# A cross network's first layer as one sequence of twelve half-blocks

## Chip, cores, metric

One core of one Trainium2 chip. The metric is the device time of one execution in microseconds (us), as the median of several runs; lower is better.

## The reference

A cross network of six layers over a batch of 4096 rows with 416 features, all in bf16:

```
x = x0                                   # (4096, 416)
for l in range(6):
    x = x0 * (x @ ws[l] + bs[l]) + x     # ws[l]: (416, 416), bs[l]: (416,)
```

Each layer is a product with a 416 x 416 matrix, a bias, a product with the input x0 and a sum with the layer's own input.

## The kernel before

**Tiling.** The 416 features are three blocks of 128 (`NK`, the index `m` for outputs and `k` for inputs) and a remainder of 32. In the first five layers features lie on the partitions and batch rows on the free axis. The batch is two halves `s` of 2048 rows, each of four groups `g` of 512 columns; two groups make a half-block `h` (1024 columns). `XM[0]` holds x0 transposed (three blocks), `XR[0]` its remainder with the four groups `g` at partitions 32g, and `XRd` a copy of `XR[0]` with the upper and the lower 64 partitions exchanged. `XM[1]`, `XM[2]`, `XR[1]`, `XR[2]` take the layers' outputs in turn.

**Forms of product on TensorE.** A full matmul has 128 x 128 weights and 512 columns (L233). A row-tiled product has 32 input rows (the remainder) and 128 outputs; four of them, at the four groups of 32 rows of the array, run side by side (L240, L206). A column-tiled product has 128 input rows and 32 outputs; again four run side by side (L200, L212, L217). The kernel writes the place in the array as `tile_position`.

**The first layer** (`first_layer(s)`, L227 to L291), called for each half of the batch. A half-block of one feature block `m` needs 3 full matmuls (k = 0 to 2) for each of its two groups (`full`) and 2 row-tiled products (`row`). They accumulate in one PSUM tile of two banks; the pool has four such tiles. `pa` are the three half-blocks with h = 0, `pb` those with h = 1. In each half of the batch the row-tiled products come at two places: eight of them after `pa` is filled, four at the end. The remainder outputs (`mm_rem`, 16 column-tiled products per half) come at the end of the second half.

An evicted half-block goes through ACT (bias added, PSUM to a buffer `t` in SBUF, six buffers, L173), then VectorE (times x0, L180; plus the layer's input, L183).

**What is loaded, and how.** SP's queue issues eight transposing DMAs for x0 (`load_x0t`, L75), one for each group of 512 rows, then the other weights. ACT's queue issues the first layer's weights (L71), the biases (L105), the remainder of the first half of x0 in four pieces (`xrig`, L83) and the remainder rows of the first layer's weights (`WR`, L91). L111 is a small activation that has ACT load its function table. Two copies on ACT (L115) and one on GpSimd (L117) spread `WR` to the other groups of partitions. `xrig` is transposed on TensorE (`x0_rem0`, L159) and copied by VectorE to `XR[0]` and `XRd`. The remainder of the second half (`xrem`, 2048 pieces of 64 bytes, L88) is loaded later: `load_xrem1` is called at the end of `x0_rem0`, and a one-column memset of `xrem` on VectorE (L86), behind those copies, holds the load back. VectorE transposes `xrem` into `XR[0]` (L167) and fills `XRd` by two copies (L169), in `x0_rem1`.

**Order.** A scheduler orders the instructions of each engine from the program's order and its own estimates. `pin(...)` keeps an instruction in the program's order on its engine. Each DMA takes one of eight semaphores in turn, and waits until the transfer that had it before has landed.

**After the first layer,** layers 1 to 4 run over six tiles each (`mm_full`, `mm_row`, L200 and L206) with one pair of remainder products per layer; the last layer puts the batch on the partitions (L365 to L392) and stores the outputs.

Of the kernel before, what the change touches and what calls it, by code (L numbers as in the profile page):

```python
# [9 lines left out]
ACT = mybir.ActivationFunctionType  # L10
ALU = mybir.AluOpType
BF16 = mybir.dt.bfloat16
# [4 lines left out]
def kernel(  # L17
# [7 lines left out]
    nc = tc.nc  # L25
    B, D = x0.shape
    L = ws.shape[0]
    P = 128
# [38 lines left out]
    def col0(s, g):  # L67
        return SW * s + CW * g
# [8 lines left out]
    def pin(ins):  # L77
        tc.keep_in_program_order(ins)
# [4 lines left out]
                nc.scalar.dma_start(xrig[:, i, :].rearrange("p (g r) -> p g r", g=NG), x0_v[:, i:16:4, NK * P:D])  # L83

    def load_xrem1():
        pin(nc.vector.memset(xrem[:, 0, 0:1], 0.0))  # L86
        with nc.allow_non_contiguous_dma(reason="64B row segments"):
            pin(nc.scalar.dma_start(xrem[:], x0[SW:2 * SW, NK * P:D].rearrange("(p t) r -> p t r", p=P)))  # L88

# [18 lines left out]
    load_x0t(0, 1)  # L108
    load_xrem0()
    load_wr0()  # L110
    nc.scalar.activation(dz[:, 1:2], dz[:, 0:1], ACT.Identity, bias=dz[:, 0:1], scale=1.0)  # L111
    for g in range(1, NG):
        dst, src = WR[32 * g:32 * g + 32, 0, :], WR[0:R, 0, :]
        if g < NG - 1:
            nc.scalar.copy(dst, src)  # L115
        else:
            nc.gpsimd.tensor_copy(dst, src)  # L117
    for g in range(2, NG):
        load_x0t(0, g)
    load_x0t(1, 0)  # L120
# [17 lines left out]
    fill_wd(0, 1)  # L138
    fill_wd(1, L)

    wps = psum.tile([P, CW], FP32, tag="ps", name="wps")

# [13 lines left out]
    def x0_rem0(tpr):  # L156
        nc.tensor.transpose(tpr[:, CW:CW + L], bsb[0:L, NK * P:4 * P], ident[0:L, 0:L])
        for i in range(4):
            nc.tensor.transpose(tpr[:, 128 * i:128 * i + 128], xrig[:, i, :], ident[:])  # L159
        for dst, src in ((slice(0, P), slice(0, P)), (slice(64, P), slice(0, 64)), (slice(0, 64), slice(64, P))):  # L160
            to = XR[0] if dst == src else XRd
            pin(nc.vector.tensor_copy(to[dst, 0:CW], tpr[src, 0:CW]))
        nc.vector.tensor_copy(bR[:], tpr[:, CW:CW + L])
        load_xrem1()

    def x0_rem1():
        pin(nc.vector.transpose(XR[0][:, CW:2 * CW].rearrange("p (j t) -> p t j", t=16), xrem[:]))  # L167
        for dst, src in ((slice(64, P), slice(0, 64)), (slice(0, 64), slice(64, P))):
            pin(nc.vector.tensor_copy(XRd[dst, CW:2 * CW], XR[0][src, CW:2 * CW]))  # L169

    def ew_act(n, pt, bias):
        t = tpool.tile([P, 2 * CW], BF16, name="t")
        nc.scalar.activation(t[:, 0:n], pt, ACT.Identity, bias=bias, scale=1.0)  # L173
        return t

    def ew_main(l, s, m, h, pt, cur, nxt, pin_all=False, t=None):
        c0 = col0(s, 2 * h)
        if t is None:
            t = ew_act(2 * CW, pt[:].rearrange("p a b -> p (a b)"), bM[:, m, l:l + 1])
        prod = nc.vector.tensor_tensor(out=t[:], in0=t[:], in1=XM[0][:, m, c0:c0 + 2 * CW], op=ALU.mult)  # L180
        if pin_all:
            pin(prod)
        total = nc.vector.tensor_tensor(out=nxt[:, m, c0:c0 + 2 * CW], in0=t[:], in1=cur[:, m, c0:c0 + 2 * CW], op=ALU.add)  # L183
        if pin_all and s:
            pin(total)

    def ew_rem(l, s, pr, curR, nxtR, pin_all=False, t=None):
        tr = ew_act(CW, pr, bR[:, l:l + 1]) if t is None else t
        prod = nc.vector.tensor_tensor(out=tr[:, 0:CW], in0=tr[:, 0:CW], in1=XR[0][:, CW * s:CW * s + CW], op=ALU.mult)  # L189
        if pin_all:  # L190
            pin(prod)
        total = nc.vector.tensor_tensor(out=nxtR[:, CW * s:CW * s + CW], in0=tr[:, 0:CW], in1=curR[:, CW * s:CW * s + CW], op=ALU.add)  # L192
        if pin_all:
            pin(total)

    def mm_full(l, s, m, g, pts, cur, first, last):
        c0 = col0(s, g)
        for k in range(NK):
            for q in range(4):
                nc.tensor.matmul(pts[g // 2][32 * q:32 * q + 32, g % 2, :], lhsT=WM[:, l, k, 128 * m + 32 * q:128 * m + 32 * q + 32],  # L200
                                 rhs=cur[:, k, c0:c0 + CW], start=(first and k == 0), stop=(last and k == NK - 1),
                                 tile_position=(0, 32 * q))

    def mm_row(l, s, m, pts, curR, first, last):
        for g in range(NG):
            nc.tensor.matmul(pts[g // 2][:, g % 2, :], lhsT=WR[32 * g:32 * g + 32, l, 128 * m:128 * m + 128],  # L206
                             rhs=curR[32 * g:32 * g + 32, CW * s:CW * s + CW],
                             start=first, stop=last, tile_position=(32 * g, 0))

    def mm_rem(l, s, pr, cur, curR):  # L210
        for g in range(NG):
            nc.tensor.matmul(pr[32 * g:32 * g + 32, :], lhsT=WD[:, l, g, :], rhs=curR[:, CW * s:CW * s + CW],  # L212
                             start=True, stop=False, tile_position=(0, 32 * g))
        for k in range(NK):
            for g in range(NG):
                c0 = col0(s, g)
                nc.tensor.matmul(pr[32 * g:32 * g + 32, :], lhsT=WM[:, l, k, NK * P:D], rhs=cur[:, k, c0:c0 + CW],  # L217
                      start=False, stop=(k == NK - 1), tile_position=(0, 32 * g))

    def new_pts():  # L220
        return [psum.tile([P, 2, CW], FP32, tag="ps", name=f"pt{h}") for h in range(2)]
# [2 lines left out]
        nc.sync.dma_start_transpose(out=XLrows[:, 16 * s:16 * s + 16, 128 * k:128 * k + 128],  # L224
                                    in_=nxt[:, k, SW * s:SW * s + SW])

    def first_layer(s):  # L227
        cur, curR, nxt, nxtR = XM[0], XR[0], XM[1], XR[1]

        def full(pt, m, h, gl, after_row):  # L230
            c0 = col0(s, 2 * h + gl)
            for k in range(NK):
                nc.tensor.matmul(pt[:, gl, :], lhsT=WM[:, 0, k, 128 * m:128 * m + 128], rhs=cur[:, k, c0:c0 + CW],  # L233
                                 start=(k == 0 and not after_row), stop=(k == NK - 1 and after_row))

        def row(pt, m, h, opens):
            for gl in range(2):
                rg = 32 * ((2 * h + gl) ^ (2 if m == 1 else 0))
                src = XRd if m == 1 else curR
                nc.tensor.matmul(pt[:, gl, :], lhsT=WR[rg:rg + 32, 0, 128 * m:128 * m + 128],  # L240
                                 rhs=src[rg:rg + 32, CW * s:CW * s + CW],
                                 start=opens, stop=not opens, tile_position=(rg, 0))

        def ph(m):
            return psum.tile([P, 2, CW], FP32, tag="ps", name=f"ph{m}")

        pa = [ph(m) for m in range(NK)]
        if s == 0:
            for m in range(NK):
                full(pa[m], m, 0, 0, False)  # L250
            tp0 = psum.tile([P, CW + 8], BF16, tag="ps", name="tpr")
            x0_rem0(tp0[:])
            for m in range(NK):
                full(pa[m], m, 0, 1, False)
        else:
            for gl in range(2):
                for m in range(NK):
                    full(pa[m], m, 0, gl, False)
        pb = [ph(0)]
        row(pa[0], 0, 0, False)  # L260
        row(pb[0], 0, 1, True)
        row(pa[2], 2, 0, False)
        row(pa[1], 1, 0, False)
        for m in range(NK):
            ew_main(0, s, m, 0, pa[m], cur, nxt, pin_all=(s == 1))
        for m in range(NK):
            if m:
                pb.append(ph(m))
            for gl in range(2):
                full(pb[m], m, 1, gl, m == 0)  # L270
        row(pb[1], 1, 1, False)
        row(pb[2], 2, 1, False)
        if s == 0:
            x0_rem1()
            for m in range(NK):
                ew_main(0, s, m, 1, pb[m], cur, nxt, pin_all=True)
            return
        pr = psum.tile([P, 2, CW], FP32, tag="ps", name="pr")
        for r in range(NS):
            mm_rem(0, r, pr[:, r, :], cur, curR)  # L280

        def act_main(m):
            return ew_act(2 * CW, pb[m][:].rearrange("p a b -> p (a b)"), bM[:, m, 0:1])

        tb, tr = [act_main(0), act_main(1)], [ew_act(CW, pr[:, 0, :], bR[:, 0:1])]
        tb.append(act_main(2))
        tr.append(ew_act(CW, pr[:, 1, :], bR[:, 0:1]))
        ew_rem(0, 0, None, curR, nxtR, True, tr[0])
        for m in range(NK):
            ew_main(0, s, m, 1, None, cur, nxt, True, tb[m])  # L290
        ew_rem(0, 1, None, curR, nxtR, True, tr[1])  # L291

    bias_setup()
    pe_filler(1, CW)
    for s in range(NS):
        first_layer(s)

    def rem_pair(l, cur, curR, nxtR, feeds_last):
        pr2 = psum.tile([P, 2, CW], FP32, tag="ps", name="pr2")
# [154 lines left out]
```

## Time and profile before

| | |
|---|---|
| runs | 130.0, 130.21, 130.25 us; median 130.21 |
| profiled execution | 130.03 us, of which its span is 128.2 us |
| granted TensorE clock, mean | 0.995 |
| x0 transposes issued by SP | 0.73 to 17.1 us |
| first matmul on x0 | 5.61 us |
| row-tiled products of the first layer start | 10.57, 15.19, 19.51, 24.04 us |
| first matmul of layer 1 | 26.11 us |
| first eviction of the first layer on ACT | 11.00 us |

Times in the profile count from the start of the span. A line of a group names the source line, the engine and the operation. The clock that the array was granted is full all through but for the last slices. Matmuls are pipelined, so one takes 0.38 us while its neighbours start 0.216 us apart.

### The profile page before, as it was taken

The numbers are of one execution on the slowest core, as the hardware profiler recorded it, in microseconds if no ns is written. First come the engines' busy times: TensorE is split into PE (matmuls) and PEld (weight loads), VectorE is DVE, ScalarE is ACT, GpSimd is POOL, SyncE is SP. The second block draws the span as 40 slices with busy tenths as digits, with TensorE's granted clock in tenths as the row PEclk, the third lists the DMA queues.
The fourth block names the chain that finished last, engine by engine and source line by source line (L and its number), as shares of the span: only waits on it lengthen the run. The fifth ranks groups of instructions, "written<-read, shape, count | busy, mean of one in ns | idle before, by whom it ended". The sixth has DMA issues, their size and how long they took to land.

```text
span 128.2 us, 3995 instructions
## 1 busy us (share of the span) xinstructions
PE 122.7 (96%) x1698; PEld 55.1 (43%) x1698; DVE 108.1 (84%) x196; ACT 86.8 (68%) x99; POOL 5.5 (4%) x18
## 2 busy tenths in 40 slices
PE   7999999999999999999999999999999999999960
PEld 3344343444344444434444434444434445445420
DVE  0033999999999999999999989898989899898991
ACT  0138857878496658857658857658857897569670
POOL 4004000700000000000000000000000000000000
PEclk9999999999999999999999999999999999999997
DMA  3999999999960000000000000000297899987754
GB/s 93 248 233 196 193 222 251 279 332 332 337 202 0 5 0 8 0 0 5 0 5 0 5 0 5 0 0 5 48 160 165 161 134 240 182 269 248 224 183 136
DMA packets 42230, 16.38 MB, mean 128 GB/s; under 512 B 31034, under 2 KB 42212, under 8 KB 42212
## 3 DMA queue, kind: packets, MB, share of 16 engines
q1 hardware_dynamic: 37432, 15.40, 52.8%
q10 hardware_dynamic: 4780, 0.72, 3.7%
q8 instruction: 13, 0.21, 0.7%
q14 instruction: 5, 0.04, 0.1%
HBM read 6.15 MB, written 3.41 MB: 75 GB/s over the span
## 4 chain that ended last, share of the span: by engine, by line
PE 81%; DVE 6%; DMA 6%; ACTq 2%; issue 1%; SPq 1%; ACT 1%; DVEq 0%
PE pt L200 50%; PE ph L233 11%; PE pt L206 5%; PE pr L217 5%; PE py L365 4%; DMA xrig<-in_x_dram 4%; DVE t L393 4%; DVE o L382 2%; DMA out_dram<-o 2%; PE pr L212 2%; PE ph L240 1%; PE py L360 1%; ACTq L83 1%; SPq L383 1%; PE py L371 1%
## 5 line engine op out<-in xcount | busy, mean ns | idle before, releaser
L200 PE MATMUL pt<-XM,WM 128*32 128x512 bf16 x1152 | 65.2, 379 | 0.0
L173 ACT ACTIVATE t<-pt,bM 128x1024 bf16<-128x1024 f32 x48 | 49.6, 1115 | 17.7 <-PE pt L206 17.7
L183 DVE TENSOR_TENSOR XM<-t,XM 128x1024 bf16<-128x1024 bf16 x60 | 41.5, 692 | 3.6
L180 DVE TENSOR_TENSOR t<-t,XM 128x1024 bf16<-128x1024 bf16 x60 | 41.4, 689 | 3.5 <-ACT t L173 3.4
L200 PEld LDWEIGHTS <-WM 128*32 128x32 bf16 x1152 | 29.7, 97 | 33.8 <-issue 5.1
L392 ACT CAST t<-py 128x416 bf16<-128x416 f32 (+1 forms) x23 | 14.8, 643 | 4.7 <-PE py L365 2.5
L233 PE MATMUL ph<-XM,WM 128*128 128x512 bf16 x72 | 16.4, 379 | 0.3 <-DMA XM<-in_x_dram 0.3
L365 PE MATMUL py<-WM,XM 128*128 128x416 bf16 x90 | 16.5, 339 | 0.0
L173 ACT ACTIVATE t<-ph,bM 128x1024 bf16<-128x1024 f32 x12 | 12.6, 1113 | 3.5 <-PE ph L240 3.5
L365 PEld LDWEIGHTS <-XM 128*128 128x128 bf16 x90 | 8.5, 98 | 7.8 <-issue 1.4
L393 DVE TENSOR_TENSOR t<-t,X0rows 128x416 bf16<-128x416 bf16 (+1 forms) x23 | 10.4, 456 | 1.1 <-ACT t L392 1.1
L233 PEld LDWEIGHTS <-WM 128*128 128x128 bf16 x72 | 6.8, 98 | 8.8 <-issue 1.3
L382 DVE TENSOR_TENSOR o<-t,XLrows 128x416 bf16<-128x416 bf16 (+1 forms) x23 | 10.4, 455 | 0.0
L173 ACT ACTIVATE t<-pr,bR 128x512 bf16<-128x512 f32 x10 | 6.4, 685 | 2.9 <-PE pr L217 2.9
L217 PE MATMUL pr<-XM,WM 128*32 128x512 bf16 x120 | 8.2, 379 | 0.0
L206 PE MATMUL pt<-XR,WR 32*128 32x512 bf16 x96 | 7.3, 379 | 0.0
L111 ACT ACT_TABLE_LOAD x1 | 1.3, 1283 | 6.0 <-DMA XM<-in_x_dram 6.0
L192 DVE TENSOR_TENSOR XR<-t,XR 128x512 bf16<-128x512 bf16 x10 | 4.2, 424 | 0.7
L217 PEld LDWEIGHTS <-WM 128*32 128x32 bf16 x120 | 3.2, 97 | 3.2
L145 PE MATMUL wps<-const-float32-1.0 128*128 128x512 f32 x4 | 3.6, 1044 | 0.8 <-PEq L438 0.8
L189 DVE TENSOR_TENSOR t<-t,XR 128x512 bf16<-128x512 bf16 x10 | 4.2, 419 | 0.0
L154 DVE CAST bM<-pb 128x18 f32<-128x18 bf16 x1 | 0.2, 177 | 4.5 <-PE pb L153 4.5
(42 smaller groups left out, 36.7 us busy)
## 6 DMA issues: line engine op xcount, KB each, us to landing
X0rows<-in_x_dram SPq DMA_DIRECT2D x8, 312.0 KB, 7.1
out_dram<-o SPq DMA_DIRECT2D x9, 208.0 KB, 4.2
WM<-in_ws_dram SPq DMA_DIRECT2D x5, 312.0 KB
out_dram<-o SPq DMA_DIRECT2D x13, 104.0 KB, 1.7
X0rows<-in_x_dram SPq DMA_DIRECT2D x4, 208.0 KB, 6.1
WR<-in_ws_dram SPq DMA_DIRECT2D x4, 130.0 KB, 5.2
WM<-in_ws_dram ACTq DMA_DIRECT2D x1, 312.0 KB
XM<-in_x_dram SPq DMA_TRANSPOSE x8, 5.6
```

The lines of the kernel that those rows point to most:

```text
L173: nc.scalar.activation(t[:, 0:n], pt, ACT.Identity, bias=bias, scale=1.0)
L180: prod = nc.vector.tensor_tensor(out=t[:], in0=t[:], in1=XM[0][:, m, c0:c0 + 2 * CW], op=ALU.mult)
L183: total = nc.vector.tensor_tensor(out=nxt[:, m, c0:c0 + 2 * CW], in0=t[:], in1=cur[:, m, c0:c0 + 2 * CW], op=ALU.add)
L189: prod = nc.vector.tensor_tensor(out=tr[:, 0:CW], in0=tr[:, 0:CW], in1=XR[0][:, CW * s:CW * s + CW], op=ALU.mult)
L200: nc.tensor.matmul(pts[g // 2][32 * q:32 * q + 32, g % 2, :], lhsT=WM[:, l, k, 128 * m + 32 * q:128 * m + 32 * q + 32], rhs=cur[:, k, c0:c ...
L206: nc.tensor.matmul(pts[g // 2][:, g % 2, :], lhsT=WR[32 * g:32 * g + 32, l, 128 * m:128 * m + 128], rhs=curR[32 * g:32 * g + 32, CW * s:CW ...
L217: nc.tensor.matmul(pr[32 * g:32 * g + 32, :], lhsT=WM[:, l, k, NK * P:D], rhs=cur[:, k, c0:c0 + CW], start=False, stop=(k == NK - 1), tile ...
L233: nc.tensor.matmul(pt[:, gl, :], lhsT=WM[:, 0, k, 128 * m:128 * m + 128], rhs=cur[:, k, c0:c0 + CW], start=(k == 0 and not after_row), sto ...
L365: nc.tensor.matmul(py[:, 0:D], lhsT=cur[:, k, q_cols(q, g)], rhs=WM[:, l, k, :], start=((not closes) and k == 0), stop=(closes and k == NK ...
L382: tc.keep_in_program_order(nc.vector.tensor_tensor(out=o, in0=t, in1=xl, op=ALU.add))
L392: nc.scalar.copy(tv, src)
L393: tc.keep_in_program_order(nc.vector.tensor_tensor(out=tv, in0=tv, in1=X0rows[:, b, :], op=ALU.mult))
```

## The change

- The first layer becomes one function without the loop over halves: twelve half-blocks in one sequence, `pa[0..2]`, `pb[0..2]` (first half of the batch), `qa[0..2]`, `qb[0..2]` (second half).
- Row-tiled products come at three places of eight: behind `pa` (as before); behind the full matmuls of `pb[1]`, `pb[2]` and of the first groups of `qa[0]`, `qa[1]`; and behind those of `qa[2]` and `qb[0]`, where they open `qb[1]` and `qb[2]`.
- `qb[1]` and `qb[2]` are column-tiled (`cols`): 24 products of 32 outputs for each, in place of 6 full matmuls. The remainder products follow them.
- `load_xrem1` loses its memset and is called right behind the small activation, ahead of the copies of `WR`. The activation and the copies are pinned.
- `x0_rem1` (transpose of `xrem` and two copies) moves ahead of VectorE's work on `pa[1]` and `pa[2]`.
- Evictions are issued one by one (`act_main`, `act_rem`), all pinned, and the remainder's evictions come behind all others. The matmuls of the first layer from the first row-tiled place on, those of its remainder, and the first tile of layer 1 are pinned.

In the order of instructions that comes out, ACT's queue holds the table load, the small activation, the load of `xrem` (waiting on the semaphore of the first `xrig` load), then the copies of `WR`. SP's list is the same but for the semaphores of three transposes and of the loads behind them. TensorE has 36 products more.

The core of the diff:

```diff
     def load_xrem1():
-        pin(nc.vector.memset(xrem[:, 0, 0:1], 0.0))
...
-    nc.scalar.activation(dz[:, 1:2], dz[:, 0:1], ACT.Identity, bias=dz[:, 0:1], scale=1.0)
-    for g in range(1, NG):
-        dst, src = WR[32 * g:32 * g + 32, 0, :], WR[0:R, 0, :]
...
+    pin(nc.scalar.activation(dz[:, 1:2], dz[:, 0:1], ACT.Identity, bias=dz[:, 0:1], scale=1.0))
+    load_xrem1()
...
+        copy_wr0()
         for dst, src in ((slice(0, P), slice(0, P)), (slice(64, P), slice(0, 64)), (slice(0, 64), slice(64, P))):
...
-        load_xrem1()
...
-    def first_layer(s):
+    def first_layer():
...
+        def cols(pt, s, m, h, gl):
+            c0 = col0(s, 2 * h + gl)
+            for k in range(NK):
+                for q in range(4):
+                    pin(nc.tensor.matmul(pt[32 * q:32 * q + 32, gl, :], lhsT=WM[:, 0, k, 128 * m + 32 * q:128 * m + 32 * q + 32],
+                                         rhs=cur[:, k, c0:c0 + CW], start=False, stop=(k == NK - 1), tile_position=(0, 32 * q)))
...
+        row(pa[0], 0, 0, 0, ())
+        row(pb[0], 0, 0, 1, (0, 1))
+        row(pa[2], 0, 2, 0, ())
+        row(pa[1], 0, 1, 0, ())
+        dve_main(0, 0, 0, act_main(pa[0], 0))
+        x0_rem1()
+        for m in range(1, NK):
+            dve_main(0, m, 0, act_main(pa[m], m))
+        for gl in range(2):
+            full(pb[0], 0, 0, 1, gl, False)
+        dve_main(0, 0, 1, act_main(pb[0], 0))
+        for m in range(1, NK):
+            pb.append(ph(m))
+            for gl in range(2):
+                full(pb[m], 0, m, 1, gl, True)
+        qa = [ph(m) for m in range(2)]
+        for m in range(2):
+            full(qa[m], 1, m, 0, 0, True)
+        row(pb[1], 0, 1, 1, ())
+        row(pb[2], 0, 2, 1, ())
+        row(qa[0], 1, 0, 0, (1,))
+        row(qa[1], 1, 1, 0, (1,))
+        for m in range(1, NK):
+            dve_main(0, m, 1, act_main(pb[m], m))
+        for m in range(2):
+            full(qa[m], 1, m, 0, 1, False)
+            dve_main(1, m, 0, act_main(qa[m], m))
+        qa.append(ph(2))
+        for gl in range(2):
+            full(qa[2], 1, 2, 0, gl, True)
+        qb = [ph(0)]
+        for gl in range(2):
+            full(qb[0], 1, 0, 1, gl, True)
+        qb += [ph(m) for m in range(1, NK)]
+        row(qa[2], 1, 2, 0, ())
+        row(qb[0], 1, 0, 1, ())
+        row(qb[1], 1, 1, 1, (0, 1))
+        row(qb[2], 1, 2, 1, (0, 1))
+        ta, tb = act_main(qa[2], 2), [act_main(qb[0], 0)]
+        for m in range(1, NK):
             for gl in range(2):
+                cols(qb[m], 1, m, 1, gl)
+            tb.append(act_main(qb[m], m))
         pr = psum.tile([P, 2, CW], FP32, tag="ps", name="pr")
+        tr = []
         for r in range(NS):
             mm_rem(0, r, pr[:, r, :], cur, curR)
+            tr.append(act_rem(r))
         ew_rem(0, 0, None, curR, nxtR, True, tr[0])
+        dve_main(1, 2, 0, ta)
         for m in range(NK):
+            dve_main(1, m, 1, tb[m])
         ew_rem(0, 1, None, curR, nxtR, True, tr[1])
```

More of the change, by code (lines that the diff above doesn't have):

```diff
@@ L136, in fill_wd, with copy_wr0 @@
             nc.gpsimd.tensor_copy(WD[32 * g:32 * g + 32, l0:l1, g, :], WR[32 * g:32 * g + 32, l0:l1, NK * P:D])
-    fill_wd(0, 1)
-    fill_wd(1, L)
+    def copy_wr0():
+        for g in range(1, NG):
+            dst, src = WR[32 * g:32 * g + 32, 0, :], WR[0:R, 0, :]
+            if g < NG - 1:
+                pin(nc.scalar.copy(dst, src))
+            else:
+                nc.gpsimd.tensor_copy(dst, src)
+        fill_wd(0, 1)
+        fill_wd(1, L)
     wps = psum.tile([P, CW], FP32, tag="ps", name="wps")
@@ L225, in xl_dmat, with ph, full, row @@
                                     in_=nxt[:, k, SW * s:SW * s + SW])
-    def first_layer(s):
+    def first_layer():
         cur, curR, nxt, nxtR = XM[0], XR[0], XM[1], XR[1]
-        def full(pt, m, h, gl, after_row):
+        def ph(m):
+            return psum.tile([P, 2, CW], FP32, tag="ps", name=f"ph{m}")
+        def full(pt, s, m, h, gl, opens, held=True):
             c0 = col0(s, 2 * h + gl)
             for k in range(NK):
-                nc.tensor.matmul(pt[:, gl, :], lhsT=WM[:, 0, k, 128 * m:128 * m + 128], rhs=cur[:, k, c0:c0 + CW],
-                                 start=(k == 0 and not after_row), stop=(k == NK - 1 and after_row))
-        def row(pt, m, h, opens):
+                mm = nc.tensor.matmul(pt[:, gl, :], lhsT=WM[:, 0, k, 128 * m:128 * m + 128], rhs=cur[:, k, c0:c0 + CW],
+                                      start=(opens and k == 0), stop=(not opens and k == NK - 1))
+                if held:
+                    pin(mm)
+        def cols(pt, s, m, h, gl):
[4 more added lines that the diff above has]
+                                         rhs=cur[:, k, c0:c0 + CW], start=False, stop=(k == NK - 1), tile_position=(0, 32 * q)))
+        def row(pt, s, m, h, opens):
             for gl in range(2):
@@ L239, in row @@
                 src = XRd if m == 1 else curR
[L240 to L245, printed above, removed]
-        pa = [ph(m) for m in range(NK)]
[L248 to L255, printed above, removed]
-            for gl in range(2):
-                for m in range(NK):
-                    full(pa[m], m, 0, gl, False)
@@ L259, in first_layer @@
[L259 to L268, printed above, removed]
-            for gl in range(2):
[L270 to L277, printed above, removed]
+                pin(nc.tensor.matmul(pt[:, gl, :], lhsT=WR[rg:rg + 32, 0, 128 * m:128 * m + 128],
+                                     rhs=src[rg:rg + 32, CW * s:CW * s + CW],
+                                     start=gl in opens, stop=gl not in opens, tile_position=(rg, 0)))
@@ new lines, in act_main, with act_rem, dve_main @@
+        def act_main(pt, m):
+            t = tpool.tile([P, 2 * CW], BF16, name="t")
+            pin(nc.scalar.activation(t[:], pt[:].rearrange("p a b -> p (a b)"), ACT.Identity, bias=bM[:, m, 0:1], scale=1.0))
+            return t
+        def act_rem(r):
+            t = tpool.tile([P, 2 * CW], BF16, name="t")
+            pin(nc.scalar.activation(t[:, 0:CW], pr[:, r, :], ACT.Identity, bias=bR[:, 0:1], scale=1.0))
+            return t
+        def dve_main(s, m, h, t):
+            ew_main(0, s, m, h, None, cur, nxt, True, t)
@@ new lines, in first_layer @@
+        pa = [ph(m) for m in range(NK)]
+        for m in range(NK):
+            full(pa[m], 0, m, 0, 0, True, held=False)
+        tp0 = psum.tile([P, CW + 8], BF16, tag="ps", name="tpr")
+        x0_rem0(tp0[:])
+        for m in range(NK):
+            full(pa[m], 0, m, 0, 1, True, held=False)
+        pb = [ph(0)]
+        row(pa[0], 0, 0, 0, ())
[3 more added lines that the diff above has]
+        dve_main(0, 0, 0, act_main(pa[0], 0))
@@ L294 @@
     pe_filler(1, CW)
-    for s in range(NS):
-        first_layer(s)
+    first_layer()
     def rem_pair(l, cur, curR, nxtR, feeds_last):
```

37 lines of the change are left out of this document (17 added, 20 removed).

## The prediction

> **What bounds the kernel now.** I read the busy shares first, then the chain of work that ended last, then the gaps between matmul starts.
>
> ```profile
> PE 122.7 (96%) x1698; PEld 55.1 (43%) x1698; DVE 108.1 (84%) x196; ACT 86.8 (68%) x99; POOL 5.5 (4%) x18
> ...
> PE   7999999999999999999999999999999999999960
> ```
>
> TensorE is busy nearly throughout. The chain (start us, length, work) shows its stretch in the first layer:
>
> ```profile
> 8.10 0.45 PE tpr L159 x2
> 8.55 2.09 PE ph L233 x9
> 10.64 0.62 PE ph L240 x8
> 11.27 3.99 PE ph L233 x18
> 15.26 0.33 PE ph L240 x4
> 15.58 3.99 PE ph L233 x18
> 19.57 0.54 PE ph L240 x8
> 20.12 3.99 PE ph L233 x18
> 24.11 0.33 PE ph L240 x4
> 24.44 0.33 PE pr L212 x4
> 24.77 0.65 PE pr L217 x12
> 25.41 0.22 PE pr L212 x4
> 25.63 0.65 PE pr L217 x12
> 26.28 2.59 PE pt L200 x48
> ```
>
> The pieces touch from 8.10 to 111.42: nothing but matmuls, so what is saved on TensorE is saved, and what TensorE waits is lost. The L240 lines are the row-tiled products; there are four such places. After 111.42 the chain runs through ACT, VectorE and the output stores, all released by TensorE, so a shift carries to the end.
>
> Next, who feeds the second half. From the timeline (start, length):
>
> ```profile
> 9.51 1.10 ACT L115 COPY WR<-WR 32x416 bf16<-32x416 bf16 x2 [1.96 <-DMA WR<-in_ws_dram]
> 10.14 0.64 ACTq L88 DMA_DIRECT2D xrem<-in_x_dram  x1
> ...
> 16.42 2.36 DVE L167 STREAM_TRANSPOSE XR<-xrem 128x512 bf16<-128x512 bf16 x1 [0.19 <-DMA xrem<-in_x_dram]
> 18.81 0.61 DVE L169 COPY XRd<-XR 64x512 bf16<-64x512 bf16 x2
> ```
>
> The remainder load takes 6.3 us from issue to landing, and VectorE already waits 0.19 for it. And what the load does to the others: the packets of SP's queue (q1, the x0 transposes) in one microsecond alone (9.2 to 10.2), then in one shared with xrem on ACT's queue q10 (14.2 to 15.2):
>
> ```profile
> q1 hardware_dynamic: 1133, 0.29, 127.5%
> ...
> q1 hardware_dynamic: 765, 0.20, 99.0%
> q10 hardware_dynamic: 521, 0.03, 35.9%
> ```
>
> **The change part by part.**
>
> *Fewer turns of the array.* Starts of successive full matmuls are 0.216 us apart. Between a full matmul and the first row-tiled one it is 0.312 (15.189 after 14.877), so the turn costs 0.096; from the last row group to the next full one 0.317, then 0.227 in place of 0.216: 0.112. A group of four row products is 0.216 whatever its place. Before, the 24 row products take four places of 8, 4, 8 and 4; after, three of 8. Six groups stay six groups; one turn in and one out go: 0.096 + 0.112 = 0.21 us. The last turn, from rows to column tiles, stays: before it led to L212 (0.314 - 0.216 = 0.098), after to the column-tiled half-blocks.
>
> A rule of the Trainium skill prices this lower: the page "TensorE: Matmul & The Clock Gate", Part 2, "Step-by-step: what each phase is for", puts the drain of the array at about 128 cycles, which the next matmul hides. As an estimate from that page and its 2.4 GHz, two unhidden drains are 0.11 us. The rows say 0.21, and I use the rows.
>
> *Two half-blocks column-tiled.* 12 full matmuls become 48 column tiles. Groups of four at L200 are 0.216 apart (48 in 2.59 us), the same as one full matmul: nothing. They now run into L212 in the same tiling.
>
> *Evictions.* ACT needs 1.03 us per half-block, TensorE 1.29. Four PSUM tiles turn over. From 11.198, the new second place starts after 24 full matmuls: 11.198 + 0.011 + 24 x 0.2158 + 0.096 = 16.48. ACT evicts pb[1] from about 16.95 to 18.06, and qa[2], which takes its tile, starts at 17.01 + 0.011 + 6 x 0.2158 = 18.32; 0.26 spare. The tightest later one: qb[2] opens in the third place at 21.2 and wants qa[1] evicted, 21.06. Fine, though not by much. The six t buffers: ACT's eviction of qb[2] near 24.5 wants the product of pb[2] done, near 23.6. Fine. The remainder evictions move behind all main ones; layer 1 needs the first at its row products, 28.6, and VectorE has it by 27.4.
>
> *VectorE's order.* Its transpose of xrem and the two copies (3.0 us) move ahead of the products of pa[1] and pa[2] (L180 and L183, 2.66 us for the two). Total work is the same less one memset (0.06). If xrem is late, those four instructions queue behind the wait; their readers (t buffers, layer 1 at 25.9) have a microsecond, so only TensorE's second place matters. There the rows of qa[1] start at 16.48 + 0.22 = 16.70 and want the transpose (2.36) and the first copy (0.30). So xrem must have landed by 16.70 - 0.05 - 0.30 - 0.03 - 2.36 = 13.96.
>
> *The load moved.* Before, it is issued at 10.14, when VectorE's memset frees it, and lands at 16.39. After, it stands behind L111's ACTIVATE on ACT's queue and waits for the first xrig load (landed at 1.91 + 4.1 = 6.0). How early it goes, the trace brackets only: at 6.0 if the queue runs ahead of ACT (at 10.14 it issues while the copy of 10.08 is running, so it can), at 7.55 if it waits for the ACTIVATE to end (7.25 + 0.29). By its 6.25 us the load lands at 12.3 to 13.8, in time for 13.96, though the later by only 0.15. The WR copies behind it on ACT want WR (landed 9.49) anyway: covered if the 0.64 of issue ends before that, and each microsecond later would be one on place one.
>
> What is in its way is the transpose of x0 group 3 (first half). Landing marks in the trace: group 2 at 9.67, group 3 at 11.31; TensorE reads group 3 at 11.198 + 0.011 + 3 x 0.2158 = 11.86. Slack 0.55. Group 3's packets run from 9.0 to 10.45. xrem's packets first show 1.95 after its issue; issued at 7.55, from 9.5. The remaining 0.95 us of group 3 stretch by 1133/765 = 1.48, so 0.46 later: 11.77, 0.09 to spare. Issued at 6.0 the packets come behind WR's (8.4 to 8.9): all 1.45 us stretch, 0.70 later: 12.01, a stall of 0.15. Later transposes gain: xrem is out of their way.
>
> *Queues.* SP issues the same list; three of its transposes wait on other loads than before, all landed by 9.7, before 10.2. GpSimd keeps its order.
>
> **The sum.** Profiled execution: 130.03 (span 128.2 and 1.8 around it). 130.03 - 0.21 = 129.82. The runs before have a median of 130.21, 0.18 above their profiled one, so 130.00 beside it. What a measurement of this kernel can tell from no change is about 0.2%, 0.26 us; my 0.21 lies just inside, and three runs spread by 0.25.
>
> **The rivals.**
>
> *Group 3 late (slower).* Point of decision: xrem's packets earlier than 9.3. For it: the queue's running ahead, and the transpose of group 1 of the second half, which shared with xrem and took 6.4 us to land where the one before took 4.1. Price: from 0.15 (above); if all 2048 packets of xrem pass first, they displace 2048 x (1133 - 765) / 521 = 1450 transpose packets, 1.28 us, so group 3 is 0.73 beyond its slack and the net is +0.52: 130.73. Middle, a stall of 0.5: +0.29, 130.50. Against: 13 of 16 DMA engines finish group 3 by 10.87, so most have 0.4 more.
>
> The Trainium skill's page "DMA: Bandwidth & Descriptors", "Queues, rings and completion order", speaks for this rival: an engine takes turns between its queues, packet by packet. Equal turns would halve q1's 1133 where 765 were seen; as an estimate from that rule even the late issue stalls 12.26 - 11.86 = 0.40 and gives 130.40.
>
> *xrem late at the second place.* Point: landing after 13.96. WR's load first showed packets 2.8 us after its issue, xrem's 1.95; at 2.8 from 7.55 it lands 0.85 later, 14.65, and stalls 0.7: net +0.48, 130.69. Against: an early issue removes it, and it and the first rival exclude each other.
>
> *More than the sum.* In place one the second pair of row products starts 0.085 after the first, behind ACT's second WR copy (ends 10.61). If the new order ends that gap: -0.30, 129.91. Against: the copies start when WR lands.
>
> *Not as said.* The scheduler could undo the sequence, leaving four places: 130.2. The new order of instructions on TensorE shows three places, so this is nearly out.
>
> **Chances.** Forecast, clean -0.21: 0.52, which the spread of runs divides into 0.28 faster and 0.24 the same. More: 0.10 (0.09, 0.01). Group 3 late: 0.23 (0.07 the same, 0.16 slower). xrem late: 0.11 (0.03, 0.08). Anything else, undoing included: 0.04 (0.01, 0.03). Faster 0.37, same 0.36, slower 0.27. The clean case alone is 129.85 to 130.15; 8 in 10 need the late cases to their ends and the better one with its spread: 129.7 to 130.7.
>
> **What would show it.** Right: three runs of row products in the chain, a full one 0.216 after its neighbour all through, layer 1 starting at 25.9 in place of 26.1. Wrong: a gap on TensorE before the fourth matmul after place one (group 3), or between the row groups of place two (xrem); both name their DMA. The issue time of xrem decides between them.

## The result, and the profile after

| | before | after |
|---|---|---|
| runs | median 130.18 us (130.0 to 130.25) | median 131.87 us (131.72 to 131.92) |
| ratio to before, 95% interval | | 1.013 (1.0112 to 1.0147) |
| profiled execution, span | 130.03, 128.2 | 131.72, 129.9 |
| first matmul of layer 1 | 26.11 | 27.81 |

The change makes the kernel 1.3% slower; 130.0 was forecast, and even the dearest case of the range, 130.7, is passed. The whole loss is there when layer 1 begins: its first matmul comes 1.70 us later, and the span is 1.7 longer. The busy shares of the page after say nothing of it; TensorE is about as busy as before (95% for 96%):

```profile
PE 123.6 (95%) x1733; PEld 55.5 (43%) x1734; DVE 108.3 (83%) x195; ACT 86.7 (67%) x99; POOL 5.3 (4%) x18
```

The chain of work that ended last (start, length, work) says it. Before, it was nothing but matmuls from 8.10 on. After:

```profile
6.81 5.75 DMA XM<-in_x_dram
12.55 0.04 issue
12.60 1.02 PE ph L245 x4
13.62 0.05 issue
13.67 3.62 PE ph L245 x16
17.29 0.54 PE ph L261 x8
17.83 3.99 PE ph L245 x18
21.82 0.38 PE ph L261 x4
...
25.19 1.12 ACT t L267
26.32 0.59 ACT t L272
26.91 0.04 issue
26.95 0.40 PE pr L221 x4
27.35 0.65 PE pr L226 x12
27.99 2.59 PE pt L201 x48
```

L245 are the full matmuls, L261 the row-tiled ones, L254 the column-tiled half-blocks, L221 and L226 the remainder products, L201 layer 1. Two links are new. At 12.55 the chain comes from an x0 transpose (group 3 of the first half). At 26.91 it comes from ACT: the main evictions (L267), then the first eviction of the remainder (L272), then only the second group of remainder products. TensorE's own timeline shows the hole; the bracket is the idle time before the group and who ended it:

```profile
24.89 0.39 PE L221 MATMUL pr<-XR,WD 128*32 128x512 bf16 x4
25.11 0.82 PE L226 MATMUL pr<-XM,WM 128*32 128x512 bf16 x12
26.95 0.40 PE L221 MATMUL pr<-XR,WD 128*32 128x512 bf16 x4 [1.01 <-ACT t L272]
```

The first group would have made room for the second at 25.11 + 0.65 = 25.76; the second starts at 26.95. That is 1.19 us (1.01 is only what the modelled ends of the pipelined matmuls leave of it). The waits on TensorE between 24 and 31 us name one pair:

```profile
PE pr L221 <- ACT t L272: 1.0, 1, 1.0
```

What ACT does meanwhile:

```profile
22.19 4.13 ACT L267 ACTIVATE t<-ph,bM 128x1024 bf16<-128x1024 f32 x4 [0.41 <-PE ph L261]
26.19 0.71 ACT L272 ACTIVATE t<-pr,bR 128x512 bf16<-128x512 f32 x1
```

Four main evictions follow one another from 22.19 on (about 1.03 each). The remainder's eviction stands behind them and ends at 26.9. In the program the two groups of remainder products write the two banks of one PSUM tile `pr`, and `act_rem(0)`, which reads the first bank, stands between them. So the second group, a writer of the tile, waits for a reader of it. The chain's stretch of ACT is ACT working off a queue that TensorE had never had to wait for.

**Where 1.70 us went**, from the starts of successive matmuls in both traces (a matmul that runs freely starts 0.216 after its neighbour):

| place | before | after | difference |
|---|---|---|---|
| start of place one's full matmuls (second group of nine) | 8.54 | 8.68 | +0.14 |
| place one, first row product to next full matmul | 10.573 to 11.198: 0.625 | 10.720 to 11.714: 0.994 | +0.37 |
| group 3, start of its first matmul | 0.216 after its neighbour | 0.440 after it (12.596) | +0.22 |
| second remainder group | none | waits from 25.76 to 26.95 | +1.19 |
| all else up to layer 1 | 14.91 | 16.09 - 0.22 - 1.19 = 14.68 | -0.23 |

The rows add up to 1.70 but for rounding. I take the first for scatter of the start: the other kernels below begin this place anywhere from 8.56 to 9.16. The last row is the saving, forecast as -0.21.

The second and the third row belong to the load of `xrem`. ACT's queue issues it at 6.30, while ACT itself is still loading its table:

```profile
6.07 1.28 ACT L110 ACT_TABLE_LOAD   x1 [6.07 <-DMA XM<-in_x_dram]
6.30 0.62 ACTq L87 DMA_DIRECT2D xrem<-in_x_dram  x1
...
10.03 1.10 ACT L136 COPY WR<-WR 32x416 bf16<-32x416 bf16 x2 [2.37 <-DMA WR<-in_ws_dram]
```

Its packets fall on 9.06 to 11.50. Packets by queue between 9.0 and 9.5 us (count, MB, share of 16 engines), before:

```profile
q1 hardware_dynamic: 576, 0.14, 128.1%
```

and after:

```profile
q10 hardware_dynamic: 932, 0.06, 128.4%
q1 hardware_dynamic: 113, 0.02, 21.8%
```

The transposes on q1 nearly stop for half a microsecond; between 9.11 and 9.46 the trace has 796 packets of the load in a row, 50 for each engine if they are spread evenly, and not one of a transpose. After that the two queues take turns, packet for packet (10.4 to 10.9 us):

```profile
q1 hardware_dynamic: 372, 0.10, 84.5%
q10 hardware_dynamic: 371, 0.02, 51.3%
```

Group 3's 1536 packets of 256 bytes begin at 9.46 instead of 8.99 and take 2.20 us instead of 1.37. Not all of that is the turns: between 9.9 and 10.3 one of these packets takes 42 to 56 ns instead of 18. `WR` lands at 10.00 instead of 9.49, so ACT's copies start later and the second pair of row products in place one comes 0.455 after the first (0.085 before); group 3 lands at 12.55 instead of 11.31. These two waits are not separate prices. TensorE can't pass the fourth matmul after place one before group 3 has landed, so the 0.37 at place one only takes from the wait that would stand there otherwise: in the first kernel below place one is as short as 0.54, and the wait at group 3 is 0.58.

### The profile page after: what moved, and what is told of

Its sections match the earlier page's. It is cut to its first block, busy times and chain, and to the rows that moved or that the text cites. A ratio compares the mean times of both kernels' runs of the same rounds, so it can differ in the third digit from the quotient of the medians.

```text
span 129.9 us, 4069 instructions
## 1 busy us (share of the span) xinstructions
PE 123.6 (95%) x1733; PEld 55.5 (43%) x1734; DVE 108.3 (83%) x195; ACT 86.7 (67%) x99; POOL 5.3 (4%) x18
## 4 chain that ended last, share of the span: by engine, by line
PE 76%; DVE 6%; SPq 5%; DMA 4%; ACT 3%; issue 3%; DVEq 0%; ACTq 0%
PE pt L201 49%; PE py L411 7%; PE ph L245 7%; PE pt L209 5%; SPq L75 5%; PE pr L226 4%; DMA XM<-in_x_dram 4%; DVE t L439 4%; ACT t L267 2%; DVE o L428 2%; PE pr L221 2%; PE py L417 1%; PE py L406 1%; PE ph L261 1%; PE py L420 1%
## 5 line engine op out<-in xcount | busy, mean ns | idle before, releaser
L201 PE MATMUL pt<-XM,WM 128*32 128x512 bf16 x1152 | 65.2, 379 | 0.0
L201 PEld LDWEIGHTS <-WM 128*32 128x32 bf16 x1152 | 29.9, 97 | 33.7 <-issue 5.1
L267 ACT ACTIVATE t<-ph,bM 128x1024 bf16<-128x1024 f32 x12 | 12.4, 1116 | 2.8 <-PE ph L261 2.8
L245 PE MATMUL ph<-XM,WM 128*128 128x512 bf16 x59 | 13.7, 379 | 0.1
L439 DVE TENSOR_TENSOR t<-t,X0rows 128x416 bf16<-128x416 bf16 (+1 forms) x23 | 10.3, 453 | 1.1 <-ACT t L438 1.1
L428 DVE TENSOR_TENSOR o<-t,XLrows 128x416 bf16<-128x416 bf16 (+1 forms) x23 | 10.3, 451 | 0.0
L245 PEld LDWEIGHTS <-WM 128*128 128x128 bf16 x60 | 5.6, 98 | 7.2 <-issue 1.2
L226 PE MATMUL pr<-XM,WM 128*32 128x512 bf16 x120 | 8.2, 379 | 0.0
L174 ACT ACTIVATE t<-pr,bR 128x512 bf16<-128x512 f32 x8 | 5.1, 684 | 2.1 <-PE pr L226 2.1
L221 PE MATMUL pr<-XR,WD 128*32 128x512 bf16 x40 | 3.9, 380 | 1.0 <-ACT t L272 1.0
L226 PEld LDWEIGHTS <-WM 128*32 128x32 bf16 x120 | 3.2, 97 | 3.1
```

What stands on the lines that cost most here:

```text
L201: mm = nc.tensor.matmul(pts[g // 2][32 * q:32 * q + 32, g % 2, :], lhsT=WM[:, l, k, 128 * m + 32 * q:128 * m + 32 * q + 32], rhs=cur[:, k, ...
L226: held(nc.tensor.matmul(pr[32 * g:32 * g + 32, :], lhsT=WM[:, l, k, NK * P:D], rhs=cur[:, k, c0:c0 + CW], start=False, stop=(k == NK - 1), ...
L245: mm = nc.tensor.matmul(pt[:, gl, :], lhsT=WM[:, 0, k, 128 * m:128 * m + 128], rhs=cur[:, k, c0:c0 + CW], start=(opens and k == 0), stop=( ...
L267: pin(nc.scalar.activation(t[:], pt[:].rearrange("p a b -> p (a b)"), ACT.Identity, bias=bM[:, m, 0:1], scale=1.0))
L428: tc.keep_in_program_order(nc.vector.tensor_tensor(out=o, in0=t, in1=xl, op=ALU.add))
L439: tc.keep_in_program_order(nc.vector.tensor_tensor(out=tv, in0=tv, in1=X0rows[:, b, :], op=ALU.mult))
```

## The experiments

Two theories stood at first for the large gap: that the shared tile is to blame, or that ACT's pinned order is, in that the remainder's evictions stand behind all others. The load made a second question: how much it costs, and whether it could go early without cost. "e1 plus" below means that a kernel contains the edit of the first experiment too.

### Remainder products first, evictions behind them

```diff
         for r in range(NS):
             mm_rem(0, r, pr[:, r, :], cur, curR)
+        for r in range(NS):
             tr.append(act_rem(r))
```

> Changed kernel, but both groups of remainder products are issued before either eviction of them. Theory A (the second group waits for ACT to have read the first, since both halves are one PSUM tile): the 1.19 us gap on TensorE between L226 and the second L221 goes, layer 1 starts 1.2 us earlier, 131.87 - 1.2 = 130.7. Theory B (ACT is simply behind with its evictions, and TensorE meets that backlog wherever it next needs ACT): the gap moves to the first tiles of layer 1, and the time stays at 131.6 to 131.9.

130.89 us against 130.22 before on the same chip, ratio 1.0045 (1.0029 to 1.006). From the chain of this kernel:

```profile
25.02 0.22 PE pr L221 x4
25.23 0.65 PE pr L226 x12
25.88 0.22 PE pr L221 x4
26.10 0.65 PE pr L226 x12
26.74 2.59 PE pt L201 x48
...
35.17 0.33 PE pt L209 x4
35.50 0.03 issue
35.52 0.40 PE pt L209 x4
```

The four pieces touch; the gap is gone, though ACT evicts in the same order as in the changed kernel. About 1.0 us comes back, not 1.19: a wait of 0.19 has appeared at 35.52, in layer 1. There row products want `XR` from VectorE:

```profile
PEld L209 <- DVE XR L193: 0.3, 1, 0.3
```

and VectorE had stood idle for the first remainder eviction, because its product comes ahead of those of `qa[2]` and `qb` in the program:

```profile
27.52 0.43 DVE L190 TENSOR_TENSOR t<-t,XR 128x512 bf16<-128x512 bf16 x1 [1.19 <-ACT t L272]
```

That order is the changed kernel's too; there the gap before had hidden it. The eviction itself starts late, at 26.80, for ACT has waited 0.53 for the second group of products: the shared tile works in this direction too.

### The order kept, a PSUM tile for each remainder group

```diff
-        pr = psum.tile([P, 2, CW], FP32, tag="ps", name="pr")
         for r in range(NS):
-            mm_rem(0, r, pr[:, r, :], cur, curR)
-            tr.append(act_rem(r))
+            pr = psum.tile([P, 2, CW], FP32, tag="ps", name=f"pr{r}")
+            mm_rem(0, r, pr[:, 0, :], cur, curR)
+            tr.append(act_rem(pr))
```

> Changed kernel with products and evictions in turn as there, but each group of remainder products in a PSUM tile of its own. Theory A: the wait comes of the shared tile, so the gap goes as in the kernel with both products first, near 130.7. If the order of issue alone makes the wait, it stays: 131.9.

130.62 us in one run (before: 130.22). The products run through (second group at 25.86, 0.86 after the first at 25.00), and layer 1 starts at 26.72. The first remainder eviction starts at 26.28 instead of 26.80, and the wait of 0.19 in layer 1 is not there. Instructions, order and pins are those of the changed kernel; only the tile is no longer shared. So the wait is for the tile's first reader, not something that the order on ACT brings by itself.

### The same eviction put into the kernel before

```diff
-        for r in range(NS):
-            mm_rem(0, r, pr[:, r, :], cur, curR)
...
-        tb, tr = [act_main(0), act_main(1)], [ew_act(CW, pr[:, 0, :], bR[:, 0:1])]
+        tb, tr = [act_main(0), act_main(1)], []
+        mm_rem(0, 0, pr[:, 0, :], cur, curR)
+        tr.append(ew_act(CW, pr[:, 0, :], bR[:, 0:1]))
+        mm_rem(0, 1, pr[:, 1, :], cur, curR)
```

> Kernel before, with one edit: the first remainder eviction is issued between the two groups of remainder products. Theory A: the second group (25.24 before) now waits until the first has been evicted (27.0 before), so a gap of about 1.7 us appears there and the time is near 131.9. Theory B: nothing is waited for that was not before, 130.2.

130.71 us in one run, against 130.22: the wait is there, but much smaller than expected. Nothing of layer 1 is pinned in this kernel, and the scheduler put nine of its products between the two groups. What is left is a start 0.544 after the neighbour, 0.33 more than a free one; from the end of place one to layer 1's row products it is 0.55 more than before (11.33 to 29.49, against 11.20 to 28.80). The ninth product stands alone there, without the three that run beside it elsewhere. The wait follows the edit, then; its size depends on what may run meanwhile.

### The changed kernel without the pins around the gap

```diff
-                if (l, s, m) == (1, 0, 0):
-                    pin(mm)
...
         def held(mm):
-            if l == 0:
-                pin(mm)
+            pass
```

> Changed kernel, with the remainder products of the first layer and the first tile of layer 1 not pinned. The scheduler then puts 9 products of layer 1's first tile between the two groups of remainder products. Theory A (the second group waits for ACT's read of the first; what stands between covers the wait): 2 of the 1.19 us' groups of 0.216 are covered, and the gap shrinks to about 0.7: 131.3 to 131.5. If the pins do not matter: 131.9.

131.79 us in one run (before: 130.17), where 131.3 to 131.5 was expected. The nine products did move into the gap, and the second remainder group starts 0.753 after its neighbour instead of 1.393; this execution began place one's full matmuls at 9.16, 0.48 later than the changed kernel's, which hides the gain. From the end of place one to layer 1's row products it takes 18.47 instead of 18.80, though its wait at group 3 is 0.10 longer. So in the matmul starts the pins are worth about 0.4 of the 1.19, the two whole groups that were expected; the time of one run can't confirm it.

### The early load alone, in the kernel before

```diff
     def load_xrem1():
-        pin(nc.vector.memset(xrem[:, 0, 0:1], 0.0))
...
-    nc.scalar.activation(dz[:, 1:2], dz[:, 0:1], ACT.Identity, bias=dz[:, 0:1], scale=1.0)
+    pin(nc.scalar.activation(dz[:, 1:2], dz[:, 0:1], ACT.Identity, bias=dz[:, 0:1], scale=1.0))
+    load_xrem1()
```

(the copies of `WR` are pinned, as in the change; the call at the end of `x0_rem0` goes)

> Kernel before, with one edit: the remainder load behind the small activation as in the changed kernel, no memset. Theory A: the load is issued at 6.3, its packets delay the weights' remainder (WR, 10.0 for 9.5) and the x0 transpose of group 3 (12.5 for 11.3); TensorE waits about 0.36 in the first place and 0.22 at group 3, 130.7 to 130.8. Rival (the later start of TensorE in the changed kernel's first 11 us was chance of that one execution, such as its fillers running slower): 130.2 and no such gaps.

130.76 us against 130.22, ratio 1.0039 (1.0025 to 1.0053): the load by itself costs half a microsecond. Both its places are seen on TensorE: place one takes 10.65 to 11.81 (1.15 instead of 0.63), its second pair late,

```profile
11.27 0.40 PE L239 MATMUL ph<-XR,WR 32*128 32x512 bf16 x4 [0.17 <-POOL WD L136]
```

which the waits put down to the `WR` copy on ACT:

```profile
PEld L239 <- ACT WR L115: 0.5, 1, 0.5
```

and the first matmul of group 3 starts 0.27 late. `WR` landed at 10.10, group 3 at 12.69.

### e1 plus a load held back to 7.7 us

```diff
+    pin(nc.scalar.copy(xrem[:, 0, 0:1], ident[:, 0:1]))
     load_xrem1()
```

A one-column copy into `xrem` keeps the load behind the activation's end. By the prediction's sum for the late end of its bracket this makes group 3 just in time.

> The kernel with both products first (130.89), and a one-column copy into xrem on ACT behind the small activation, which holds the remainder load until about 7.7 (6.0 to 6.3 without). The prediction's model of the transfers (packets 1.95 after issue, sharing stretches a transpose by 1.48): group 3 lands by 11.9 and TensorE does not wait for it, xrem lands at 13.9 and the second place waits at most 0.1: 130.3. Rival (the descriptors of the load hold up those of SP's next transpose wherever they are made, as 9.0 to 9.5 in the changed kernel, when the transposes' queue nearly stood still): group 3 stays at 12.3 to 12.5, 130.7 to 130.9.

130.87 us against 130.17, ratio 1.0047 (1.0031 to 1.0063): nothing gained over the first experiment, and group 3 is later than ever, landed at 12.90:

```profile
PE ph L246 <- DMA XM<-in_x_dram: 0.7, 1, 0.7
```

The packets between 10.4 and 11.2 show where it was held up:

```profile
q10 hardware_dynamic: 1611, 0.10, 138.4%
q1 hardware_dynamic: 97, 0.02, 13.6%
```

From 10.5 to 11.3 the load has the engines almost to itself. All but ten of group 3's packets of 256 bytes were through by 10.5; but the small ones of 4 bytes, 32 of which end this transpose in the trace, came from 11.22 on, behind the burst. In the kernel before they came at 10.3 to 10.4. (What follows on q1 is thin there without any load, 116 packets from 10.4 to 10.9 in the kernel before.) A transfer whose data is through has not landed. `WR`, on the other hand, landed at 9.69, and place one was nearly as before.

### e1 plus the load on SP's queue

```diff
-            pin(nc.scalar.dma_start(xrem[:], x0[SW:2 * SW, NK * P:D].rearrange("(p t) r -> p t r", p=P)))
+            nc.sync.dma_start(xrem[:], x0[SW:2 * SW, NK * P:D].rearrange("(p t) r -> p t r", p=P))
...
-    load_xrem1()
     for g in range(2, NG):
         load_x0t(0, g)
+    load_xrem1()
     load_x0t(1, 0)
```

> The kernel with both products first (130.89), and the remainder load on SP's queue, between the transposes of groups 3 and 4, in place of ACT's queue. Theory A (the cost at group 3 and at WR is the load's running ahead of them): WR lands at 9.5 and group 3 at 11.3 as before the change, xrem by 13 to 14, group 4 by 15 (needed at 15.9); TensorE has no gap up to layer 1, which starts at 25.9 to 26.1; what is left is the 0.2 at 35.5. 130.1 to 130.3. Rival (in line it delays the second half's transposes by its own 1.3 to 2 us beyond their slack): gaps at 15.9 to 20, 130.6 and more.

130.75 us (130.3 to 131.13) against 130.17, ratio 1.0036 (1.0023 to 1.0049). Group 3 is undisturbed (landed 11.03) and `xrem` in time (13.03), but the transposes behind it are later: group 4 lands at 14.96 instead of 12.93, and a wait for the last transpose stands at 20.6. What SP's queue carries first, the others pay for. The profiled execution, the quickest, still has the 0.19 of layer 1; where the slower ones lose more, no trace shows.

### e1 plus the load as before

```diff
     def load_xrem1():
+        pin(nc.vector.memset(xrem[:, 0, 0:1], 0.0))
...
-    load_xrem1()
...
         nc.vector.tensor_copy(bR[:], tpr[:, CW:CW + L])
+        load_xrem1()
```

> The kernel with both products first, with the load of xrem as in the kernel before (memset behind VectorE's copies, issue at 10.14). Group 3 and WR are as before; xrem lands at 16.4, the rows of qa in the second place want it at 13.96, so TensorE waits there 2.4 us: 130.2 - 0.2 + 2.4 = 132.4. If the sequence itself does not need the earlier load: 130.0.

132.59 us in one run (130.17). `xrem` lands at 16.56 and the second place waits:

```profile
PE ph L262 <- DVE XR L169: 2.0, 1, 2.0
```

The new sequence can't do without an earlier load: the prediction's bound, `xrem` landed by 13.96, is passed by 2.60; from the end of place one to layer 1 it takes 2.48 longer than in the two kernels without waits at the end.

### The order on VectorE, on top of the load on SP's queue

```diff
-        ew_rem(0, 0, None, curR, nxtR, True, tr[0])
         dve_main(1, 2, 0, ta)
+        ew_rem(0, 0, None, curR, nxtR, True, tr[0])
```

> The kernel with the load on SP's queue, and VectorE's product for qa[2] ahead of that for the first remainder (which in the kernel with both products first kept VectorE idle for 1.19 us, so that the second remainder's sum came late and TensorE waited 0.2 at 35.5). The clean case of the prediction: no gap on TensorE at all, 0.21 under the kernel before, 130.0. Rival: a gap at group 4 or at layer 1's rows is left, and it stays at 130.2 or above.

130.32 us against 130.17, ratio 1.0007 (0.9991 to 1.0022): no different from before. The wait in layer 1 is gone, so VectorE's order was one condition of it (the shared tile was the other: with a tile for each group it was not there either). Beside the kernel with the load on SP's queue the median is 0.43 lower, more than this wait; both kernels' runs spread by about a microsecond (0.83 and 1.14). Group 4 still comes 0.12 late, and a wait of 0.10 stands at 21.0.

### All of it, and the load issued behind group 3

Two kernels: the products first, VectorE's order, ACT's queue, and a copy on ACT that only passes time (512 or 768 columns into a scratch tile that nobody reads) ahead of the one-column copy.

```diff
+    junk = const.tile([P, 1024], BF16)
+    pin(nc.scalar.copy(junk[:, 0:512], WD[:].rearrange("p l g r -> p (l g r)")[:, 0:512]))
+    pin(nc.scalar.copy(xrem[:, 0, 0:1], ident[:, 0:1]))
     load_xrem1()
```

> The kernel with both products first, the remainder load on ACT's queue held until about 8.3 by a 512-column copy on ACT (into a scratch tile that nothing reads) ahead of the one-column copy into xrem, and VectorE's product for qa[2] ahead of the first remainder's. In the kernel held until 7.7 the load's packets began at 10.3 (2.6 after issue), just ahead of the last packets of group 3, took the engines alone until 11.25, and group 3 landed at 12.9. Theory (a burst of the load's packets holds back what is queued behind it, so only its place counts): from 8.3 the burst begins at 10.9, group 3 lands at 11.3 to 11.5 and TensorE does not wait for it; xrem lands at 13.5, in time for 13.96; no wait at 35.5: 130.0. Rival (any early issue on ACT's queue delays group 3 by a microsecond): 130.5 to 130.7.

> As the kernel held until 8.3, with a 768-column copy: issue near 8.55. Theory: the burst begins at 11.1, group 3 is free of it with more to spare, xrem lands near 13.75, with 0.2 to spare: 130.0 as well, or up to 130.2 if it lands after 13.96. Rival: 130.5 to 130.7.

| load issued | median of runs | before | ratio, 95% interval | group 3 landed | `xrem` landed |
|---|---|---|---|---|---|
| 8.22 | 130.01 us (one of 12: 713.33) | 130.17 us | 0.9981 (0.9971 to 0.9992), without that one | 11.08 | 13.24 |
| 8.72 | 129.96 us | 130.17 us | 0.998 (0.9967 to 0.9993) | 11.43 | 13.72 |

Both are a little faster than the kernel before, by 0.2%, which is what the forecast hoped for. The chain of the first:

```profile
8.57 2.10 PE ph L248 x9
10.67 0.63 PE ph L264 x8
11.29 1.62 PE ph L248 x7
12.91 0.05 issue
12.96 3.62 PE ph L248 x16
...
25.22 0.22 PE pr L224 x4
25.44 0.65 PE pr L229 x12
26.09 2.59 PE pt L204 x48
```

(lines are three further down in this kernel). The "issue" at 12.91 is no wait: two starts lie 0.432 = 2 x 0.216 apart, a record that the trace lacks; the same stands at 13.62 after. Layer 1 starts at 25.91 and the span is 128.0. From 8.57 to layer 1 TensorE waits for no DMA. The load's packets begin at 10.35, just as the 32 small packets of group 3 go out, and then run two thirds as thick as in the experiment at 7.7 (1099 for 1611), again with few of the transposes among them:

```profile
q10 hardware_dynamic: 1099, 0.07, 93.7%
q1 hardware_dynamic: 55, 0.01, 8.0%
```

(10.4 to 11.2 us). But what stands behind this burst is only group 4, which lands at 13.99 instead of 12.93 and has that time.

## Why the prediction failed

**Evictions: the step that failed.** It says "The remainder evictions move behind all main ones; layer 1 needs the first at its row products, 28.6, and VectorE has it by 27.4." It looked for the readers of what the eviction writes. It didn't look for the writers of what the eviction reads: the second group of remainder products, in the other bank of the same tile. The price it could have had from its own rows: ACT begins qb[2] "near 24.5", and with 1.03 for that and 0.69 for a remainder (as in the kernel before) it has read the first bank at 26.2. TensorE, with layer 1 at 25.9 and 0.87 for a group of remainder products, wants the second bank at 25.0. No rival covered this place, and it is 1.19 of the 1.70. Two edits remove it, each by itself: the products ahead of the eviction, or a tile for each group.

**The load: a rival in kind, mis-sized.** The prediction had a bracket of 6.0 to 7.55 for the issue, and 6.30 came: the queue runs ahead of ACT. For that end it had group 3 landing at about 12.0 and a stall of 0.15, and the clean sum held neither. Group 3 landed at 12.55, 0.69 after the 11.86 at which it was to be read. That the stall seen there is 0.22, near the 0.15, is luck: TensorE came to that place 0.51 late itself, by the 0.14 of the start and the 0.37 at place one. The term for `WR` ("landed 9.49 ... covered if the 0.64 of issue ends before that") asked about ACT's time for issuing and not about `WR`'s own packets, which came late beside the load's. In all the load costs 0.59 before place two, and half a microsecond of median by itself. That is the prediction's rival "Group 3 late", priced at 0.15 to 0.73 of stall and given a chance of 0.23; its dearest case, in which the load's packets pass first and put group 3 back by 1.28, is nearest to what came (1.24).

The way to that price holds only in part. The prediction let the transposes and the load share the engines at the mean rate seen at 14.2 to 15.2, a stretch of 1.48, by which a later issue is better. For an issue at 6.0 to 6.3 the arrangement of the packets mattered little: in the changed kernel a stretch of 0.36 us without any transpose packet came first, then turns of one packet each; in the first experiment the load passed almost in one piece, from 8.95 to 9.91; and group 3 landed at 12.55 and 12.50. At 7.70 the later issue was worse (12.90 against 12.55), since the load's packets then came in one dense stretch ahead of group 3's closing ones.

The rule weighed in the prediction belongs here. Turns of one packet each are what the trace has from 10.4 to 10.9, 372 to 371. They don't fit the 796 packets in a row of the changed kernel, nor the 1322 in a row, 83 for each engine, from 10.63 to 11.22 in the experiment at 7.7. The Trainium skill's page "DMA: Bandwidth & Descriptors", section "Queues, rings and completion order", says that an engine changes queues only between whole packets of several descriptors, 64 at most. If the trace's packets are its descriptors, the 50 or so per engine of the changed kernel agree with it; the 83 do not, unless the transposes' queue had nothing ready then. Whether the load held the transposes back in the DMA engines, or already where their packets are made, no run here tells apart.

**VectorE's order.** The prediction says "their readers (t buffers, layer 1 at 25.9) have a microsecond" of the transpose of `xrem`, and the two last kernels have no wait there. That the first remainder product of VectorE now stands ahead of three half-blocks and waits for the last evictions was not seen: 0.19 at layer 1, hidden as long as the large gap was there.

**What held.** The turns: -0.21 predicted, and -0.22 measured from place one to layer 1 in the two last kernels, where nothing waits (14.69 instead of 14.91); layer 1 starts at 25.91 in the one issued at 8.22, where the prediction said 25.9. Three places and not four, no price for column tiles, the four PSUM tiles and six buffers in time for the main half-blocks: all as said. `xrem` was needed about when the prediction said, by 13.96: landed at 16.56 it costs 2.48, which makes 14.08, and landed at 13.72 it costs nothing. The clean case, 129.85 to 130.15, is where the two last kernels lie.

## What to carry to other kernels

When an eviction is moved, look both ways: who reads what it writes, and who next writes the buffer that it reads, counting tiles as the program counts them and not banks; a wait on another engine, which the instruction order shows before any run, is to be priced and not passed over. A load that is issued earlier is not a load that is spread thinner: ask which other transfer it will meet and who waits for that one, and move it behind the packets that are needed first. When a large wait is removed, look for a small one that it had hidden, here 0.19 behind 1.19.

## What the runs showed of the hardware

- Packets of 64 bytes from one queue can pass with none of the transposes' among them: 796 in a row from 9.11 to 9.46 (issue at 6.30), 1322 in a row from 10.63 to 11.22 (issue at 7.70). In the second case a transpose whose data packets were out by 10.63 landed only at 12.90; its closing packets came from 11.22 to 11.55. With the load issued 0.5 us later, and the closing packets just ahead of its own, it landed at 11.08. What keeps the transposes back is not shown.
- At other times the same two queues take turns of one packet each: 372 and 371 from 10.4 to 10.9 in the changed kernel.
- The wait between issue and first packet of this load isn't fixed on ACT's queue: 2.0 us in the kernel before, 2.1 for the issue at 8.22, 1.9 for the one at 8.72, 2.7 to 2.8 for those at 6.30 and 7.70.
- ACT's queue issued a DMA at 6.30, 0.23 us after ACT began a table load of 1.28 us.
- The two turns of the array that the change saves cost 0.22 us together; the spacing of starts had said 0.21.
